# The four conversions in the first second product: PSUM scratch, GpSimd for the remainders, and a later, denser second attention

## The chip, the cores and the metric

The kernel runs on one NeuronCore of a Trainium2 chip. The metric is the device time of one execution in microseconds; the time before is the median of three runs. All times below are microseconds (us) unless marked ns. PE is TensorE, PEld its weight loads, DVE is VectorE, ACT is ScalarE, POOL is GpSimd, SP the queue that issues DMAs.

## The reference, cut to what matters

Causal windowed attention (window 128, linear bias per head) over 8 batches, 8 heads, 576 positions and 64 dimensions, followed by a two-layer network with a Mish activation:

```python
attn = softmax(mask(scale * q @ k.T + bias))      # per batch and head
x = (attn @ v).transpose(0, 2, 1, 3).reshape(4608, 512)
h = x @ w_in                                       # 512 -> 2048
g = h * tanh(softplus(h))                          # Mish
out = g @ w_out                                    # 2048 -> 512
```

The two weight matrices arrive as 64-bit floats, so the kernel turns their bits into 32-bit floats itself, and then splits each 32-bit value into an upper and a lower part for TensorE.

## The kernel before, in words

The rows of x are worked on in chunks: chunk c (0 to 7) is the first 512 positions of batch c, and a ninth chunk holds the remaining 64 positions of all batches. For each chunk there are two stages. The **first product** makes h in eight steps j, each with a [128, 2, 512] PSUM tile of tag `s` (two slots of two banks each), and `mish` turns it into g. The **second product** is 32 **pieces** (`second`): piece 2m+t adds six matmuls of 512 columns to the accumulator bank `po0` or `po1`; m counts 0 to 15, that is two halves of the chunk with j from 0 to 7 in each. Each m needs the two parts of g, made by `parts`: a copy on ACT (`gh`) and a subtraction on POOL (`gl`), both in a tile `gg` that has three buffers; `parts` for m is queued at piece 2m - 4.1. During the second product of chunk c the attention of batch c+1 is computed, so that x is ready when the next first product begins.

An attention is eight **units** (`unit`: a pair of heads, half of the positions), and four short `last_unit`s that go with the even ones. A unit needs one `s` slot. Its steps, with their places in slots after the unit's start: `scores` (0, PE), `exps` (0.02 and 0.25, four times DVE and then ACT), `fold` (0.7, POOL, and two tiny DVE operations), `scale` (0.95, DVE), `weights` (1.3, PE transposes and a DVE masking), `values` (1.99, PE), and for odd units `split_x` (2.02, ACT and then DVE). Units follow one another at one slot's distance; what a slot is in pieces is set by the line that the diff changes.

Every engine runs its instructions in the order in which they were written (the class `InOrder`); this order comes from sorting all steps of a stage by their place in pieces. An instruction that waits holds all that come after it on its engine.

The **conversion** of a quarter matrix (`convert_w`), in two halves a of 512 columns, is four steps: `scaled` (ACT multiplies the high words, into a scratch t), `joined` (three DVE operations on raw words, t and a scratch u: a shift, a shift with an or, a mask with an or), `upper` (ACT copies to the upper part, tile `so` or `si`) and `lower` (a subtraction, engine `last`, POOL unless told otherwise). In the first product of chunk 0 ten quarters are converted (`conv[2:12]`), with t in banks `po0` and `po1` and u in banks `w` and `o`. The last four (`conv[12:]`, the quarters o4 to o7 of w_out) are converted in the second product of chunk 0, which needs o4 in piece 8, o5 in piece 10, o6 in piece 12 and o7 in piece 14. There t lies in SBUF, in a `gg` buffer, u lies in place in the raw words, and `lower` runs on DVE. Banks `w` and `o` are used there by `last_unit` and by `values`.

The upper and lower parts of a quarter lie in the big pool of 20 slots, which are handed on in turn: the tile of quarter o4 gets the slot of raw o3, that of o5 the slot of raw o4, and so on; so `upper` of a quarter has to wait for `lower` of the quarter before it.

All instructions that go through `InOrder` show one line, L30, in the trace, so they are told apart by tile.

Of the kernel before, what the change touches and what calls it, by code (L numbers as in the profile page):

```python
# [8 lines left out]
F32 = mybir.dt.float32  # L9
F32R = mybir.dt.float32r  # L10
U32 = mybir.dt.uint32
# [5 lines left out]
P = 128  # L17
# [18 lines left out]
def attention_mish_mlp(  # L36
# [35 lines left out]
    ps = ctx.enter_context(tc.tile_pool(name="ps", bufs=1, space=bass.MemoryType.PSUM))  # L72
# [17 lines left out]
    for t in vb:  # L90
# [3 lines left out]
    pe, dve, act, pool, sp = (  # L94
        InOrder(tc, e) for e in (nc.tensor, nc.vector, nc.scalar, nc.gpsimd, nc.sync)
    )
# [7 lines left out]
    def big(name, dtype):  # L104
        return wts.tile([P, 2048], dtype, tag="w", name=name, bufs=2 * NJ + NF // 4)
# [4 lines left out]
    def load_w(kind, j):  # L110

        n = 256 if kind == "i" else DM
        if kind == "i":
            src = w_in[:, j * 256 : (j + 1) * 256].rearrange("(c p) f -> p c f", p=P)
        else:
            src = w_out[j * 256 : (j + 1) * 256, :].rearrange("(c p) f -> p c f", p=P)
        if (kind, j) == last_w:

            halves = [
                xp.tile([P, 1024], U32, tag=f"x{NCC - 2 + a}", name=f"w{kind}{j}_{a}")  # L120
                for a in range(2)
            ]
        else:
            t = big(f"w{kind}{j}", U32)
            halves = [t[:, :1024], t[:, 1024:]]
        raw_w[(kind, j)] = halves
        for a, t in enumerate(halves):
            part = src[:, a * (512 // n) : (a + 1) * (512 // n), :]
            if bits:
                load(t.rearrange("p (c n) -> p c n", n=2 * n), part.bitcast(U32))  # L130
            else:
                load(t[:, :512].bitcast(F32).rearrange("p (c n) -> p c n", n=n), part)

    def convert_w(kind, j, banks, last=pool):

        halves = raw_w.pop((kind, j))
        st = {}

        def value(a):
            return halves[a][:, 1::2].bitcast(F32) if bits else halves[a][:, :512].bitcast(F32)

        def place(a, part):
            return split[(kind, j)][:, 1024 * a + 512 * part : 1024 * a + 512 * part + 512]

        def scaled(a):  # L150
            if a == 0:
                split[(kind, j)] = big(f"s{kind}{j}", F32R)
            if not bits:
                return
            if banks:
                st[a] = ps.tile([P, 512], F32, tag=banks[a][0], name=f"t{kind}{j}_{a}")
            else:
                if a == 0:
                    st["t"] = ff.tile([P, 1024], F32, tag="gg", name=f"t{kind}{j}", bufs=3)
                st[a] = st["t"][:, 512 * a : 512 * (a + 1)]  # L160

            act.activation(st[a], value(a), AF.Copy, scale=2.0**-112)

        def joined(a):
            if not bits:
                return
            low, high, tb = halves[a][:, 0::2], halves[a][:, 1::2], st[a].bitcast(U32)
            u = high
            if banks:
                u = ps.tile([P, 512], F32, tag=banks[a][1], name=f"u{kind}{j}_{a}").bitcast(U32)  # L170
            dve.tensor_scalar(out=u, in0=tb, scalar1=3, scalar2=None, op0=ALU.logical_shift_left)
            dve.scalar_tensor_tensor(
                out=high, in0=low, scalar=29, in1=u, op0=ALU.logical_shift_right, op1=ALU.bitwise_or,
            )
            dve.scalar_tensor_tensor(
                out=high, in0=tb, scalar=0x80000000, in1=high, op0=ALU.bitwise_and,
                op1=ALU.bitwise_or,
            )

        def upper(a):  # L180
            act.activation(place(a, 0), value(a), AF.Copy)

        def lower(a):
            last.tensor_tensor(
                out=place(a, 1), in0=value(a), in1=place(a, 0).bitcast(F32), op=ALU.subtract
            )

        return scaled, joined, upper, lower

    def w_part(kind, j, part, c):  # L190
# [262 lines left out]
    def first(c, j, blocks=range(NCC)):  # L453
        if blocks[0] == 0:
            hs[j % 2] = ps.tile([P, 2, CH], F32, tag="s", name=f"h{c}_{j}", bufs=2)
        h = hs[j % 2]
        for t, cc in (
            [(t, cc) for cc in blocks for t in range(2)] if len(blocks) < NCC
            else [(t, cc) for t in range(2) for cc in blocks]
        ):  # L460
            x = xt[(c, cc)]
            for k, (w_, x_) in enumerate(((0, 0), (0, 1), (1, 0))):
                pe.matmul(
                    h[:, t, :], lhsT=w_part("i", j, w_, cc)[:, t * P : (t + 1) * P],
                    rhs=x[:, x_, :], start=(cc == 0 and k == 0), stop=(cc == NCC - 1 and k == 2),
                )
# [3 lines left out]
    def mish(c, j):  # L470
        if j % 2 == 0:
            gt[(c, j // 2)] = big(f"g{c}_{j // 2}", F32).rearrange("p (f n) -> p f n", n=CH)
        f = 2 * (j % 2)
        act.activation(gt[(c, j // 2)][:, f : f + 2, :], hs[j % 2], AF.Mish)
# [3 lines left out]
    def parts(c, half, j):  # L478

        src = gt[(c, j // 2)][:, 2 * (j % 2) : 2 * (j % 2) + 2, half * 256 : (half + 1) * 256]  # L480
        gg = ff.tile([P, 2, 2, 256], F32R, tag="gg", name=f"gg{c}_{half}_{j}", bufs=3)
        gh, gl = gg[:, 0], gg[:, 1]
        act.activation(gh, src, AF.Copy)
        pool.tensor_tensor(out=gl, in0=src, in1=gh.bitcast(F32), op=ALU.subtract)
        gs[(c, half, j)] = (gh, gl)
# [53 lines left out]
    def run(steps):  # L539
        for _, work in sorted(steps, key=lambda s: s[0]):  # L540
            work()

    def converting(weights, times, banks, last=pool):

        steps = []
        for (kind, j), at_ in zip(weights, times):
            st = []
            steps.append((at_[0], lambda kind=kind, j=j, st=st: st.extend(convert_w(kind, j, banks, last))))
            steps += [(t, lambda n=n, st=st: st[n // 2](n % 2)) for n, t in enumerate(at_)]
        return steps  # L550
# [31 lines left out]
    for c in range(B + 1):  # L582

        steps = []
        for j in range(NJ):
            if c or j:
                steps.append((j, lambda j=j: first(c, j)))
            steps.append((j + 0.9, lambda j=j: mish(c, j)))
        steps += [(NJ - 1.05, lambda j=j: parts(c, 0, j)) for j in range(2)]
        if c == 0:  # L590
            steps += converting(
                conv[2:12],
                [
                    [-0.5 + 0.84 * n + d for d in (0, 0.42, 0.3, 0.72, 0.75, 1.15, 0.8, 1.2)]
                    for n in range(10)
                ],
                (("po0", "w"), ("po1", "o")),
            )
        run(steps)
        if c == 0:  # L600
            load_w(*last_w)

        n = 4 * NJ
        steps = []
        for m in range(2 * NJ):
            for t in range(2):
                steps.append((2 * m + t, lambda m=m, t=t: second(c, *divmod(m, NJ), t)))
            if m >= 2:
                steps.append((2 * m - 4.1, lambda m=m: parts(c, *divmod(m, NJ))))
        if c == 0:  # L610
            steps += converting(
                conv[12:],
                [
                    [-0.3 + 2.0 * n + d for d in (0, 0.4, 0.7, 1.5, 1.5, 2.4, 1.9, 2.6)]
                    for n in range(4)
                ],
                None, dve,
            )
        if c + 1 < B:

            t0 = 0 if c else 5
            steps += [(t0 + (n - 2 - t0) / 9.0 * s - 0.2, f) for s, f in attention(c + 1)]
        elif c + 1 == B:
            steps.append((4.5, last_x))
        run(steps)
# [63 lines left out]
```

## Time and profile before

| What | us |
|---|---|
| Median of three runs (1044.23 to 1045.45) | 1044.44 |
| The profiled execution, its own time | 1047.03 |
| Its span, first to last instruction | 1045.3 |
| PE busy in the span | 1002.5 (96%) |
| DVE busy | 367.0 (35%) |
| ACT busy | 395.9 (38%) |
| POOL busy | 292.0 (28%) |

A busy share is a mean over the whole span. The second product of chunk 0 runs from 109.65 to 199.07 in the profiled execution, that of chunk 1 from 242.75 to 310.47.

### The profile page before, as it was taken

To read this page: it belongs to the slowest core of one execution; us is meant where nothing else is said; L and a number is where in the kernel's file an instruction comes from. 1 tells how busy PE (TensorE), PEld (TensorE's weight loads), DVE (VectorE), ACT (ScalarE), POOL (GpSimd) and SP (SyncE) were. 2 spreads that over 40 slices of the span, in tenths; PEclk is the share of its full clock that TensorE was granted. 3 is DMA by queue.
4 is the path that set the end of the run, shared out by engine and by line. 5 is a ranking of instruction groups with operands and counts; after the bars stand their busy time and mean duration, and the time that the engine had idled before them with its cause. 6 is when DMAs were issued, how large, how long until landed. Compare 5 with 4: busy or idle time off the path is not lost.

```text
span 1045.3 us, 14263 instructions
## 1 busy us (share of the span) xinstructions
PE 1002.5 (96%) x5358; PEld 789.3 (76%) x5358; DVE 367.0 (35%) x1118; ACT 395.9 (38%) x958; POOL 292.0 (28%) x286
## 2 busy tenths in 40 slices
PE   7599859999999999999999999999999999999998
PEld 5378547787778777887788777877787778888886
DVE  4879876203540255005610553035402550010000
ACT  4447645215431444234512542154314442231221
POOL 2326434103420243014400341034302430141042
PEclk9789979999999999999999999999999999999999
DMA  8950102200220012002200122003200101010001
GB/s 268 399 182 1 64 6 90 69 0 27 92 70 1 25 60 73 32 1 62 93 33 1 43 77 69 1 26 93 70 1 23 60 14 41 1 41 21 1 1 41
DMA packets 52133, 59.32 MB, mean 57 GB/s; under 512 B 13024, under 2 KB 32608, under 8 KB 52064
## 3 DMA queue, kind: packets, MB, share of 16 engines
q1 hardware_dynamic: 50880, 57.69, 17.2%
q8 instruction: 42, 0.69, 0.3%
q10 hardware_dynamic: 1184, 0.72, 0.2%
q14 instruction: 27, 0.22, 0.1%
HBM read 47.91 MB, written 10.49 MB: 56 GB/s over the span
## 4 chain that ended last, share of the span: by engine, by line
PE 83%; DVE 1%; ACT 1%; POOL 0%; issue 0%; POOLq 0%
PE po L30 36%; PE h L30 33%; PE s L30 8%; PE o L30 4%; DVE pz L30 0%; POOL gg L30 0%; PE pt_1l L30 0%; PE pt_2l L30 0%; PE pt_3l L30 0%; PE pt_0l L30 0%; ACT pz L30 0%; POOL pz L30 0%; ACT gg L30 0%; ACT x L30 0%; ACT pz_3l L30 0%
## 5 line engine op out<-in xcount | busy, mean ns | idle before, releaser
L30 PE MATMUL po<-so,gg 128*128 128x512 f32 x1728 | 430.6, 399 | 2.0 <-ACT gg L30 1.0
L30 PE MATMUL h<-x,si 128*128 128x512 f32 x1728 | 394.6, 390 | 0.0
L30 PEld LDWEIGHTS h<-x,si 128*128 128x128 f32 x1728 | 325.0, 188 | 67.7 <-issue 0.2
L30 POOL TENSOR_TENSOR gg<-g,gg 128x512 fp32r<-128x512 f32 x144 | 185.6, 1292 | 674.6 <-ACT gg L30 570.1
L30 PEld LDWEIGHTS po<-so,gg 128*128 128x128 f32 x1728 | 314.9, 188 | 75.8 <-issue 6.5
L30 DVE CUSTOM_DVE_ANT_0 pz<-s,nb 128x256 f32<-128x256 f32 (+1 forms) x256 | 84.5, 386 | 299.1 <-PE s L30 289.5
L30 ACT ACTIVATE g<-h 128x1024 f32<-128x1024 f32 x72 | 74.0, 1028 | 269.1 <-PE h L30 269.1
L30 ACT ACTIVATE pz<-pz,mx 128x256 f32<-128x256 f32 (+1 forms) x256 | 120.5, 472 | 131.2 <-DVE mx L30 131.1
L30 ACT ACTIVATE gg<-g 128x512 fp32r<-128x512 f32 x144 | 88.5, 622 | 44.7 <-PE po L30 42.8
L30 DVE TENSOR_TENSOR pz<-s,masks 128x1024 f32<-128x1024 f32 x56 | 68.5, 1223 | 21.1 <-PE s L30 21.1
L30 DVE TENSOR_TENSOR pz<-pz,s 128x512 f32<-128x512 f32 x64 | 43.8, 685 | 86.8 <-POOL pz L30 86.4
L30 POOL TENSOR_TENSOR pz<-pz 128x256 f32<-128x256 f32 x64 | 65.1, 1018 | 23.4 <-ACT pz L30 13.4
L30 PE MATMUL s<-qk 64*128 64x128 f32 (+1 forms) x448 | 57.7, 376 | 0.0
L30 PE MATMUL o<-pz,va 128*64 128x128 f32 (+1 forms) x560 | 54.9, 325 | 1.0 <-DVE pz L30 0.9
L30 PEld LDWEIGHTS o<-pz,va 128*64 128x64 f32 x560 | 33.3, 136 | 29.0 <-issue 10.9
L30 DVE COPY ob<-po 128x512 f32<-128x512 f32 x18 | 12.4, 691 | 117.3 <-PE po L30 117.3
L30 PE MATMUL s<-ident,pz 128*128 128x128 f32 x224 | 34.1, 275 | 15.5 <-DVE pz L30 14.4
L30 ACT ACTIVATION_READ_ACCUMULATOR pz<-pz,mx 128x1 f32 x256 | 47.9, 187 | 0.0
L30 PEld LDWEIGHTS s<-ident,pz 128*128 128x128 f32 x224 | 27.8, 141 | 23.5 <-ACT pz_0l L30 14.0
L30 PEld LDWEIGHTS s<-qk 64*128 64x128 f32 x448 | 33.9, 186 | 11.2 <-issue 8.2
L30 ACT ACTIVATE x<-o 128x512 fp32r<-128x512 f32 x32 | 18.8, 588 | 61.6 <-PE o L30 61.2
L30 DVE TENSOR_TENSOR x<-o,x 128x512 fp32r<-128x512 f32 x32 | 22.1, 691 | 54.1 <-ACT x L30 54.1
(122 smaller groups left out, 487.4 us busy)
## 6 DMA issues: line engine op xcount, KB each, us to landing
wi<-in_moe_w_in_dram SPq DMA_DIRECT2D x16, 512.0 KB, 10.8
wo<-in_moe_w_out_dram SPq DMA_DIRECT2D x16, 512.0 KB, 10.5
out_dram<-ob SPq DMA_DIRECT2D x32, 256.0 KB, 2.0
qk<-in_q_dram SPq DMA_DIRECT2D x28, 288.0 KB, 3.4
qk<-in_k_dram SPq DMA_DIRECT2D x28, 288.0 KB, 3.6
va<-in_v_dram SPq DMA_DIRECT2D x28, 256.0 KB, 2.8
first<-in_q_dram SPq DMA_DIRECT2D x4, 288.0 KB, 3.8
first<-in_k_dram SPq DMA_DIRECT2D x4, 288.0 KB, 3.9
```

What stands on the lines that cost most here:

```text
L30: return self.tc.keep_in_program_order(method(*args, **kwargs))
```

## The change: what it does

Three things, all in the second product of chunk 0. The four conversions get their scratch in PSUM: t in bank `w` for half 0 and bank `o` for half 1, and u in a tile of tag `s`, one for both halves; and since no engine is named for `lower`, it runs on POOL. Their places are new: a quarter every 3.05 pieces from -0.8 instead of every 2.0 from -0.3. The attention of batch 1 begins at piece 11 instead of piece 5, and since it ends at the same place, its slots are 19/9 = 2.11 pieces long instead of 25/9 = 2.78.

```diff
             if banks:
-                u = ps.tile([P, 512], F32, tag=banks[a][1], name=f"u{kind}{j}_{a}").bitcast(U32)
+                if banks[a][1] == "s":
+                    if a == 0:
+                        st["u"] = ps.tile([P, 2, 512], F32, tag="s", name=f"u{kind}{j}", bufs=2)
+                    u = st["u"][:, a, :].bitcast(U32)
+                else:
+                    u = ps.tile([P, 512], F32, tag=banks[a][1], name=f"u{kind}{j}_{a}").bitcast(U32)
...
             steps += converting(
                 conv[12:],
                 [
-                    [-0.3 + 2.0 * n + d for d in (0, 0.4, 0.7, 1.5, 1.5, 2.4, 1.9, 2.6)]
+                    [-0.8 + 3.05 * n + d for d in (0, 1.0, 0.5, 2.0, 1.9, 3.3, 2.0, 3.4)]
                     for n in range(4)
                 ],
-                None, dve,
+                (("w", "s"), ("o", "s")),
             )
         if c + 1 < B:
 
-            t0 = 0 if c else 5
+            t0 = 0 if c else 11
             steps += [(t0 + (n - 2 - t0) / 9.0 * s - 0.2, f) for s, f in attention(c + 1)]
```

The eight places in the list of a quarter are, in order: `scaled` of half 0 and 1, `joined` of 0 and 1, `upper` of 0 and 1, `lower` of 0 and 1.

## Rows read from the trace of the kernel before

**Rows 1.** Stretches: length, busy time (instructions) per engine, granted PE clock, DMA.

```profile
core 0: us, PE busy (x) PEld busy (x) DVE busy (x) ACT busy (x) POOL busy (x), PEclk, DMA share, GB/s
109.65:199.07 89.42, 71.02 (x421) 52.29 (x422) 61.04 (x161) 42.33 (x115) 31.91 (x29) 0.92 0.19 61
242.75:310.47 67.72, 67.72 (x421) 51.78 (x422) 36.31 (x126) 31.95 (x97) 26.75 (x26) 1.00 0.22 65
127.78:141.40 13.62, 0.01 (x1) 0.03 (x1) 11.73 (x30) 6.26 (x18) 2.87 (x3) 0.60 0.00 0
```

**Rows 2.** Timeline of PE: start, length, instruction, in brackets the idle time before.

```profile
111.61 5.74 PE L30 MATMUL po<-so,gg 128*128 128x512 f32 x24 [0.34 <-DVE wo L30]
...
117.28 0.93 PE L30 MATMUL s<-qk 64*128 64x128 f32 x8
...
141.40 1.09 PE L30 MATMUL s<-ident,pz 128*128 128x128 f32 x4 [13.61 <-DVE pz L30]
...
199.07 1.29 PE L30 MATMUL h<-x,si 128*128 128x512 f32 x5
```

**Rows 3.** Stretches of 2 us around PE's return; columns as in rows 1.

```profile
142.00:144.00 2.00, 2.00 (x8) 1.71 (x7) 1.23 (x8) 1.77 (x6) 0.08 (x1) 0.50 0.00 0
144.00:146.00 2.00, 2.00 (x9) 1.43 (x8) 1.56 (x2) 1.91 (x6) 1.75 (x2) 0.96 0.00 0
```

**Rows 4.** The chain that ended last, by time: the last chunk's second product.

```profile
997.22 43.53 PE po L30 x192
```

**Rows 5.** A group of DVE instructions, 78 to 112 us: count, busy us, mean ns.

```profile
L30 DVE TENSOR_SCALAR uo<-to 128x512 uint32<-128x512 uint32 x8 | 5.5, 692 | 1.1 <-ACT to L30 1.0
```

**Rows 6.** Timeline of DVE, end of the first product and of the conversions.

```profile
110.86 0.69 DVE L30 SCALAR_TENSOR_TENSOR wo<-to,wo 128x512 uint32<-128x512 uint32 x1
113.70 1.09 DVE L30 TENSOR_SCALAR wo<-to 128x512 uint32<-128x512 uint32 x1 [2.14 <-ACT to L30]
...
118.93 0.68 DVE L30 TENSOR_TENSOR so<-wo,so 128x512 fp32r<-128x512 f32 x1
...
125.17 2.38 DVE L30 TENSOR_TENSOR so<-wo,so 128x512 fp32r<-128x512 f32 x2
```

**Rows 7.** Timeline of ACT.

```profile
110.97 0.68 ACT L30 ACTIVATE so<-wo 128x512 fp32r<-128x512 f32 x1 [2.54 <-POOL so L30]
...
113.00 0.67 ACT L30 ACTIVATE to<-wo 128x512 f32<-128x512 f32 x1
...
126.54 1.28 ACT L30 ACT_TABLE_LOAD   x1
...
158.42 0.51 ACT L30 ACTIVATE pz<-pz,mx 128x256 f32<-128x256 f32 x1 [1.10 <-DVE mx L30]
...
160.41 0.62 ACT L30 ACTIVATE gg<-g 128x512 fp32r<-128x512 f32 x1
```

**Rows 8.** Timeline of POOL.

```profile
113.19 1.31 POOL L30 TENSOR_TENSOR so<-wo,so 128x512 fp32r<-128x512 f32 x1
...
125.40 1.60 POOL L30 TENSOR_TENSOR gg<-g,gg 128x512 fp32r<-128x512 f32 x1 [4.28 <-ACT gg L30]
...
161.16 1.27 POOL L30 TENSOR_TENSOR gg<-g,gg 128x512 fp32r<-128x512 f32 x1 [4.75 <-PE po L30]
162.38 1.27 POOL L30 TENSOR_TENSOR pz<-pz 128x512 f32<-128x512 f32 x1
```

**Rows 9.** Timeline of DVE: `scale` of units 2 to 5, and one `split_x`.

```profile
156.16 0.69 DVE L30 TENSOR_TENSOR pz<-pz,s 128x512 f32<-128x512 f32 x1 [2.25 <-POOL pz L30]
157.36 0.69 DVE L30 TENSOR_TENSOR x<-o,x 128x512 fp32r<-128x512 f32 x1 [0.51 <-ACT x L30]
...
163.69 0.69 DVE L30 TENSOR_TENSOR pz<-pz,s 128x512 f32<-128x512 f32 x1 [1.91 <-POOL pz L30]
...
167.93 0.67 DVE L30 TENSOR_TENSOR pz<-pz,s 128x512 f32<-128x512 f32 x1
...
177.05 0.69 DVE L30 TENSOR_TENSOR pz<-pz,s 128x512 f32<-128x512 f32 x1 [2.51 <-POOL pz L30]
```

## Prediction

> **What bounds the kernel now.** I read the busy shares first: TensorE is busy for 96% of the span, so a change pays only where PE stands still or runs slowly. Then the stretches [rows 1]: the second product of chunk 0 takes 89.42, that of chunk 1, with the same 421 products, 67.72, with PE busy throughout. So 21.70 is all that the changed stage can return. The PE timeline [rows 2] shows where most of it lies: one wait of 13.61 before the transposes of unit 0, released by DVE (`scale` of unit 0). During it PE's clock falls: a mean of 0.60 over 13.62 is full speed for about 2.7 after PE stopped and half speed, 1.2 GHz, from then on [rows 1]; after PE's return at 141.40 it stays at 0.50 until about 144 [rows 3], so some 2.7 of products run at half speed, a loss of 1.35. PE's idle time in the stage is 89.42 - 71.02 = 18.4, so there are 4.8 of other, shorter waits. 21.70 - 18.4 - 1.35 leaves about 2 of products merely drawn out around the waits.
>
> DVE explains the long wait: it is busy for 11.73 of those 13.62 [rows 1]. Its queue holds the conversions ahead of the `exps` and the `scale` of unit 0.
>
> **The change, part by part.** A piece is 43.53 / 32 = 1.36 of PE [rows 4]. An attention costs PE 67.72 - 43.53 = 24.2, or 3.0 per unit [rows 1, 4].
>
> *DVE.* With u in PSUM the three operations of `joined` have the form of the first product's: 0.69 each [rows 5, 6], 2.07 for a half, 16.6 for the eight. In the old form the shift is in SBUF; one took 1.09 at 113.70 [rows 6], while POOL was in a subtraction [rows 8]. The eight subtractions leave DVE: undisturbed 0.68, two beside POOL 2.38 together [rows 6], so some 8 in all. The start doesn't move: DVE ends the first product's work at 111.55 and waits for the first `scaled`, on ACT from 113.00 [rows 6, 7], behind an `upper` that waited 2.54 for POOL [rows 7]. DVE thus has the last `joined` done at 113.7 + 16.6 = 130.3, if nothing holds it. It needs ACT alone, whose scaled halves stay ahead: at most two copies and one `gg` of about 0.6 each come between.
>
> *POOL.* This is the new long queue. It is busy with the first product's last `lower` until 114.5 [rows 8]. Its order then is `gl` of m=2, lower, `gl` 3, lower, `gl` 4, lower, lower, `gl` 5, lower, `gl` 6, lower, `gl` 7, lower, lower, `gl` 8, `fold` of unit 0. At 1.31 for a `lower` and 1.28 for a `gl` [rows 8], with about 0.75 of waiting for the first `upper` (ready at 115.75 + 0.66), `gl` 5 is done at 125.5 and the seventh `lower` at 132.0. The eighth waits for its `upper`, which ACT has queued behind `exps` of unit 0: the seventh `upper` done at 130.1, the table load for Exp 1.28 [rows 7], four exponentials of at most 2.0 (158.42 to 160.41) [rows 7], the `upper` 0.66: about 133.9. So lower to 135.2, `gl` 8 to 136.5, `fold` of half the width to 137.2, and `scale` (0.69 [rows 9]) to 137.9.
>
> *PE.* Piece 1 starts at 111.61 as now, after a wait of 0.34 [rows 2], for a bank that the first product's conversions hold. Thirteen pieces, two `scores` (0.93 for the eight short products [rows 2]; about 1.4 with the `last_unit`'s and 1.1 for the second), and 0.8 in piece 10 for `gl` 5, give 111.61 + 17.7 + 2.5 + 0.8 = 132.6. PE has to wait there until 137.9: 5.3 in place of 13.61. This is longer than the 2.7 for which the clock held out in the old wait, so I keep its 1.35. The quarters themselves are in time: o4, o5 and o6 are wanted in the third product of pieces 8, 10 and 12, at about 121.6, 124.4 and 129.4, and their last `lower` ends at 120.4, 124.3 and 129.4; o7 is ready at 135.2, before PE's return.
>
> *Banks and transfers.* The first `s` slots come free when `mish` of the last steps has read h, before DVE needs them; `scores` of units 0 and 1 take the slots of o6's and o7's u, free by 126 and 129.6, when PE gets there. The loads of the later pairs and their v move with the units (piece 7.7 to 13.0 for the first, on SP's queue, beside the stores of pieces 14 and 15). Each lands within 4 (medians 2.8 to 3.6 in the profile's DMA issues) and is used over six pieces later, more than 8: nothing.
>
> *Shorter slots.* PE needs 2.11 x 1.36 + 3.0 = 5.9 per slot; with 2.78 it was 6.8. Against this stands a loop over engines: `scale` of one unit, then DVE's `exps` of the next, ACT, POOL's `fold`, `scale`. From unit 2 to 3 it took 163.69 - 156.16 = 7.53 [rows 9], with `split_x` (about 1.2) at its start and a `gg` copy and a `gl` (together 1.9, 160.41 to 162.38) [rows 7, 8] before the `fold`. In the new order a `gg` and `gl` stand before the `fold` of units 0 to 5. So the loop is 7.5 to units 3 and 5, about 6.3 to unit 1, 5.6 to units 2 and 4 (narrower exponentials and fold), and 1.3 to 1.9 less to units 6 and 7. PE's own slots alternate between 6.0 and 5.2, but 7.4 from unit 4 to 5, where three pieces fall, and 4.7 to unit 7. Walked through, PE waits 0.3, 1.5, 0.2, 0.1 and 0.9: 3.0.
>
> *Sum.* 0.34 + 0.8 + 5.3 + 1.35 + 3.0, and 1.0 of products drawn out (half of the 2 above, as the waits are about half), is 11.8 over the undisturbed 67.72, where it was 21.7. The stage becomes 9.9 shorter: in the profiled execution 1047.03 would become 1037.1 and the span 1035.4. The median of the runs is 1044.44, 2.6 below that execution; from it, **1034.5**.
>
> **A rule that speaks against one part.** A subtraction of two 128x512 tiles takes 1.31 on POOL [rows 8] and 0.68 on DVE [rows 6] where nothing disturbs it. The Trainium skill, GPSIMD Engine Reference, section 4.1, says the same as a rule: elementwise work on a tile belongs on VectorE, since GpSimd is about twice as slow with two inputs. By that rule the change moves eight operations the wrong way, and rival B is the result. But two subtractions on DVE beside a `gl` took 2.38 [rows 6], and the Trainium skill, SBUF — State Buffer, section "SBUF: two separate sides", explains such rows: a DVE operation with two SBUF inputs and a GpSimd operation lock each other out for a whole instruction. All new forms on DVE have an input in PSUM, and the rows of the first product show no such stretching.
>
> **The rivals.**
>
> A, *everything is covered*: `fold` and `scale` come soon after DVE's end, and the loops fit. For it: DVE is done at 130.3, and with exponentials, fold and scale (2.5 + 0.75 + 0.69) behind, unit 0 could be ready at 134.3; without a wait over 2.7 the clock stays full. Against it: the written order of ACT and POOL. Price: only 0.34, perhaps 1.7 and 1 remain, a gain of 21.7 - 3 = 18.7: **1025.7**.
>
> B, *POOL is slower, and the slots don't shorten*: each of the 14 operations ahead of `fold` takes 1.60, as one `gl` beside DVE did [rows 8], which adds 14 x 0.3 = 4.2; and two slots keep the 13.4 that units 3 to 5 took (163.69 to 177.05) [rows 9], 6.7 each over 5.9, another 5.6 for seven, less the 3.0 counted: a gain of 9.9 - 4.2 - 2.6 = 3.1, **1041.3**. Against it: the first product's `lower` keeps 1.31 beside a busy DVE, and PE itself paced the old slots most of the time.
>
> C, *slower*: the loop rules the slots and lengthens them. All that is counted apart from slots is 8.8, so the stage is slower than now once slots cost 12.9 of waits. PE's seven intervals add up to 39.7, so this is reached at a mean loop of 7.5. The loop to unit 5 took 177.05 - 167.93 = 9.1, with 2.51 of it waiting for POOL [rows 9]; if all were so, the waits would be 24 and the time 1044.4 + 11.1 = **1055.5**. Against it: PE was late in most of those loops, and the one to unit 4 took 4.2, 13.4 for both [rows 9].
>
> That the change does nothing is excluded by the same stretch: DVE's queue before unit 0 changes by some 8.
>
> **How the numbers follow.** Forecast (1030.5 to 1038) 0.58; A, towards 1025.7, 0.15; B, 1038 to 1042.4, 0.18; C or no change 0.09. The range 1025.5 to 1041.5 runs from A to B: the wait at unit 0 between 1.7 and 9.5, those of the slots between 0 and 5.6; what lies beyond is C and the tails. 0.2% is about 2.1 us, which is what a measurement of this kernel can tell from no change: 0.91 faster, 0.04 the same, 0.05 slower.
>
> **What the profile would show.** DVE's `joined` in 0.69s from 113.7 to about 130.3, without subtractions; POOL without a pause from 115 to 132; the long wait of PE at 132 to 138, before the first transposes, released by a DVE that waits for POOL; the clock down in it; the steps from one `scale` to the next near 7.5 and 5.6 in turn; the first product of chunk 1 from about 189. The prediction is wrong if PE waits earlier, for `so` of o4 to o7; if `exps` of unit 0 come much after 131; or if PE waits over 1.5 in most slots.

## The result, and the profile after

The changed kernel takes 1035.93 (median of four runs, 1034.06 to 1036.46) against 1044.91 in the runs beside it: a ratio of 0.9906, 95% interval 0.9894 to 0.9919. That is 9.0 less; the forecast was 9.9 less, 1034.5. The span of the profiled execution fell from 1045.3 to 1034.5.

The moment at which the second product of chunk 0 begins differs by up to 2.8 between the profiles of this document, and by 1.1 between two profiles of the changed kernel (109.42 and 108.34). Kernels are therefore compared below by the **stage**: from the start of piece 0 to the first product of chunk 1, on PE's timeline. It was 89.42 [rows 1]. Now, as a stretch, and stretches of 2 us in PE's wait and after it (columns as in rows 1):

```profile
109.42:188.34 78.92, 70.79 (x421) 52.67 (x422) 53.69 (x153) 42.20 (x115) 40.59 (x37) 0.98 0.22 69
...
134.00:136.00 2.00, 0.00 (x0) 0.00 (x0) 0.33 (x2) 0.51 (x1) 2.00 (x2) 1.00 0.28 93
136.00:138.00 2.00, 0.31 (x2) 0.34 (x3) 1.15 (x4) 0.48 (x2) 1.09 (x3) 0.91 0.00 0
138.00:140.00 2.00, 2.00 (x8) 1.78 (x7) 2.00 (x8) 2.00 (x9) 0.00 (x0) 0.50 0.03 8
140.00:142.00 2.00, 2.00 (x8) 1.56 (x7) 0.96 (x3) 0.52 (x1) 1.41 (x2) 0.73 0.00 0
```

The stage is 10.5 shorter; the rest of the span's 10.8 lies in its beginning. DVE has 7.4 less to do in it, POOL 8.7 more. PE's timeline after:

```profile
111.38 13.47 PE L30 MATMUL po<-so,gg 128*128 128x512 f32 x58 [0.34 <-DVE wo L30]
125.38 0.73 PE L30 MATMUL po<-so,gg 128*128 128x512 f32 x2 [0.52 <-POOL gg L30]
...
137.69 1.09 PE L30 MATMUL s<-ident,pz 128*128 128x128 f32 x4 [4.66 <-DVE pz L30]
...
138.64 4.14 PE L30 MATMUL po<-so,gg 128*128 128x512 f32 x12
...
145.48 3.00 PE L30 MATMUL po<-so,gg 128*128 128x512 f32 x12
...
158.46 0.63 PE L30 MATMUL s<-ident,pz 128*128 128x128 f32 x4 [1.28 <-DVE xo_1l L30]
...
188.34 16.94 PE L30 MATMUL h<-x,si 128*128 128x512 f32 x74
```

The wait of 13.61 [rows 2] has become 4.66, at the same transposes, and five more pieces are done before it. The granted clock stays at 1.00 through the whole wait and falls only as PE comes back. The twelve products behind it still take 4.14, where 3.00 is usual (at 145.48), since the clock is then at half until about 141. What the wait hangs on is seen on POOL and ACT:

```profile
130.34 1.29 POOL L30 TENSOR_TENSOR so<-wo,so 128x512 fp32r<-128x512 f32 x1
133.63 1.29 POOL L30 TENSOR_TENSOR so<-wo,so 128x512 fp32r<-128x512 f32 x1 [2.00 <-ACT so L30]
134.88 1.26 POOL L30 TENSOR_TENSOR gg<-g,gg 128x512 fp32r<-128x512 f32 x1
136.09 0.72 POOL L30 TENSOR_TENSOR pz<-pz 128x256 f32<-128x256 f32 x1
```
```profile
129.84 1.28 ACT L30 ACT_TABLE_LOAD   x1
...
132.91 0.64 ACT L30 ACTIVATE so<-wo 128x512 fp32r<-128x512 f32 x1
```

ACT makes the last `upper` behind the table load and four exponentials; POOL waits 2.00 for it, does the last `lower`, then `gl` of m=8, and only then the `fold` of unit 0. Two of the three DVE operations of `joined` in this stage, grouped (count, busy us, mean ns), and the same two in the kernel before; the third, the mask with an or, takes 5.5 in both:

```profile
L30 DVE TENSOR_SCALAR uo<-to 128x512 uint32<-128x512 uint32 x8 | 5.5, 692 | 2.1 <-ACT to L30 2.1
...
L30 DVE SCALAR_TENSOR_TENSOR wo<-wo,uo 128x512 uint32<-128x512 uint32 x8 | 5.5, 689 | 0.3
```
```profile
L30 DVE SCALAR_TENSOR_TENSOR wo<-wo 128x512 uint32<-128x512 uint32 x8 | 6.5, 815 | 0.3
...
L30 DVE TENSOR_SCALAR wo<-to 128x512 uint32<-128x512 uint32 x8 | 4.6, 569 | 2.1 <-ACT to L30 2.1
```

So `joined` takes 16.5 in all with its scratch in PSUM and took 16.6 before: the shift became longer on average (the 1.09 of rows 6 is the longest of eight), the shift with an or shorter. What DVE has less to do is the eight subtractions, 8.3 before.

And `scale` of units 0 to 7, on DVE, to be read against rows 9:

```profile
136.85 0.69 DVE L30 TENSOR_TENSOR pz<-pz,s 128x512 f32<-128x512 f32 x1 [2.46 <-POOL pz L30]
...
143.15 0.69 DVE L30 TENSOR_TENSOR pz<-pz,s 128x512 f32<-128x512 f32 x1 [0.73 <-POOL pz L30]
...
150.16 0.69 DVE L30 TENSOR_TENSOR pz<-pz,s 128x512 f32<-128x512 f32 x1 [1.25 <-POOL pz L30]
...
157.62 0.69 DVE L30 TENSOR_TENSOR pz<-pz,s 128x512 f32<-128x512 f32 x1 [2.44 <-POOL pz L30]
...
163.15 0.69 DVE L30 TENSOR_TENSOR pz<-pz,s 128x512 f32<-128x512 f32 x1 [1.21 <-POOL pz L30]
...
170.63 0.69 DVE L30 TENSOR_TENSOR pz<-pz,s 128x512 f32<-128x512 f32 x1 [2.45 <-POOL pz L30]
...
175.17 0.69 DVE L30 TENSOR_TENSOR pz<-pz,s 128x512 f32<-128x512 f32 x1 [0.19 <-POOL pz L30]
...
181.68 0.69 DVE L30 TENSOR_TENSOR pz<-pz,s 128x512 f32<-128x512 f32 x1 [1.23 <-POOL pz L30]
```

The steps are 6.30, 7.01, 7.46, 5.53, 7.48, 4.54 and 6.51; before each `scale` DVE waits for POOL.

### The profile page after: what moved, and what is told of

Same layout as the page of the kernel before. It is cut to its first block, busy times and chain, and to the rows that moved or that the text cites. A ratio compares the mean times of both kernels' runs of the same rounds, so it can differ in the third digit from the quotient of the medians.

```text
span 1034.5 us, 14272 instructions
## 1 busy us (share of the span) xinstructions
PE 999.0 (97%) x5358; PEld 787.4 (76%) x5358; DVE 359.5 (35%) x1110; ACT 395.7 (38%) x958; POOL 300.6 (29%) x294
## 4 chain that ended last, share of the span: by engine, by line
PE 87%; issue 3%; DVE 2%; ACT 2%; POOL 2%; POOLq 0%; DVEq 0%; ACTq 0%
PE h L30 37%; PE po L30 36%; PE s L30 8%; PE o L30 5%; ACT pz L30 1%; POOL pz L30 1%; DVE wo L30 1%; POOL gg L30 1%; POOL so L30 1%; DVE wi L30 0%; DVE pz L30 0%; DVE uo L30 0%; ACT so L30 0%; PE pt_0l L30 0%; PE pt_2l L30 0%
## 5 line engine op out<-in xcount | busy, mean ns | idle before, releaser
L30 PEld LDWEIGHTS s<-qk 64*128 64x128 f32 x448 | 33.9, 186 | 11.2 <-issue 8.2
## 6 DMA issues: line engine op xcount, KB each, us to landing
wi<-in_moe_w_in_dram SPq DMA_DIRECT2D x16, 512.0 KB, 10.8
```

The lines of the kernel that those rows point to most:

```text
L30: return self.tc.keep_in_program_order(method(*args, **kwargs))
```

## The experiments

The theory: the gain comes from DVE's shorter queue and the later begin together; what is left of the wait is POOL's queue in front of `fold`, with the clock's fall behind it; in the short slots `gl` in front of `fold` costs PE another 2.4. The rivals: POOL is the wrong home for the remainders; one part of the change does it alone; PE itself sets the pace. Each run, with the median, the ratio to the kernel before on the same chip, and the stage:

| Run | us | ratio (95%) | stage |
|---|---|---|---|
| changed kernel | 1035.93 | 0.9906 (0.9894 to 0.9919) | 78.92 |
| e1, lower on DVE | 1041.28 | 0.9967 (0.9954 to 0.9979) | 85.04 |
| e2, old conversions, late begin | 1043.64 | 0.9991 (0.9982 to 1.0) | 88.42 |
| e3, gl just behind fold | 1034.86 | 0.9904 (0.9891 to 0.9918) | 78.18 |
| e4, last upper and lower early | 1034.40 | 0.9910 (0.9896 to 0.9925) | 78.89 |
| e5, gl between the next exps | 1029.24 | 0.9853 (0.9832 to 0.9873) | 73.03 |
| e6, gl twice | 1045.22 | 0.9999 (0.999 to 1.0008) | 88.94 |
| e7, PE kept busy | 1039.24 | 0.9942 (0.993 to 0.9955) | 82.55 |
| e8, e4 and e5 together | 1028.74 | 0.9843 (0.9828 to 0.9857) | 72.21 |
| e9, PE kept busy, free bank | 1034.24 | 0.9896 (0.988 to 0.9913) | 77.46 |
| changed kernel, beside e9 | 1036.42 | 0.9918 (0.9903 to 0.9933) | 79.07 |

**e1: the remainders on DVE again.**

```diff
-                (("w", "s"), ("o", "s")),
+                (("w", "s"), ("o", "s")), dve,
```

> The changed kernel with the eight remainders (lower) of o4 to o7 on DVE again; scratch in PSUM and all places as changed. Theory (POOL is the better home while DVE's queue holds back unit 0): DVE gets 8 subtractions of 0.68 to 1.3 on top of 16.5 and waits for ACT before some, so its conversions end near 136 to 138 instead of 130, scale of unit 0 near 140 to 141 instead of 137.5, the wait of PE before the first transposes grows from 4.66 to 7 to 9; time about 1038 to 1041. Rival (elementwise work belongs on VectorE, POOL was the bound): unit 0 is ready sooner, the wait shrinks to under 3.5, time under 1034.

The stage is 6.1 longer than with POOL; PE's waits, and DVE's subtractions:

```profile
133.19 1.13 PE L30 MATMUL s<-qk 64*128 64x256 f32 x8 [1.57 <-DVE wo L30]
142.01 1.09 PE L30 MATMUL s<-ident,pz 128*128 128x128 f32 x4 [6.10 <-DVE pz L30]
```
```profile
L30 DVE TENSOR_TENSOR so<-wo,so 128x512 fp32r<-128x512 f32 x8 | 6.4, 820 | 1.7 <-ACT so L30 1.7
```

`scale` of unit 0 came at 141.2, just past the expected 140 to 141, although this stage began 1.1 earlier. The first wait grew to 6.10 only, where 7 to 9 was expected, as PE was held at three more places before it, among them the `scores` of unit 1, whose slot DVE's last `joined` still used. The time of 1041.28 is just over the expected 1038 to 1041. The rival is out: a subtraction is faster on DVE (0.82 with its neighbours' disturbance, 1.3 on POOL), and the kernel slower.

**e2: the later begin alone.** The conversions as in the old lines of the diff ahead of the prediction, `None, dve` with the old places, and t0 = 11.

> The changed kernel with the conversions of o4 to o7 as they were before (t in a gg buffer, u in place, remainders on DVE, a quarter every 2.0 pieces); only the attention's later begin and its 2.11 slots remain. Theory (PSUM scratch with POOL and the later begin are both needed): DVE's conversions end near 138 to 140, unit 0 is ready near 143 to 145, so PE waits 10 to 12 before the transposes, with 5 more pieces done than in the kernel before; time 1039 to 1043. Rival 1 (the later begin alone does it): wait under 6, time within 2 of the changed kernel's 1035.9. Rival 2 (the old conversions starve the pieces of gg buffers, as t takes them): new waits for gg of over 3 in pieces 4 to 12, time at 1044 or over.

The time is 1043.64, a gain of only 0.1%, and the upper end of its interval is at 1. Both mechanisms are in the trace: unit 0 is late (PE returns at 144.97, after a wait of 4.74 where 10 to 12 was expected), and the pieces starve, as rival 2 said, with 5.3 of waits for `gg` copies on ACT in three places, none as long as 3:

```profile
123.98 1.20 PE L30 MATMUL po<-so,gg 128*128 128x512 f32 x4 [2.08 <-ACT gg L30]
...
144.97 1.08 PE L30 MATMUL s<-ident,pz 128*128 128x128 f32 x4 [4.74 <-DVE pz L30]
```
```profile
L30 DVE TENSOR_TENSOR so<-wo,so 128x512 fp32r<-128x512 f32 x8 | 10.0, 1254 | 1.0 <-ACT so L30 0.7
```

So nearly all of the gain needs the conversions' new form. Against e2, e1 has the scratch and the new places alone, which no run separates: they take 3.4 off the stage. PE's waits for `gg` copies fall from 5.3 to 0.9, as t no longer takes `gg` buffers, and the subtractions on DVE from 10.0 to 6.4. Moving these to POOL takes off another 6.1. The other half, the new form with the old begin at piece 5, was not tried: u would take `s` slots between those of unit 0 and unit 1, and by the written order PE would come to the `scores` of unit 1 before the work that frees their slot. So that the later begin is needed as well is argued from the order, not shown by a run.

**e3: gl just behind fold.**

```diff
-                steps.append((2 * m - 4.1, lambda m=m: parts(...)))
+                at_ = 2 * m - 4.1
+                if c == 0 and m >= NJ:
+                    at_ = 10.8 + 19 / 9 * (m - NJ + 0.72)
+                steps.append((at_, lambda m=m: parts(...)))
```

> The changed kernel with the g parts (gg on ACT, gl on POOL) of the second half, m = 8 to 15, queued just behind the fold of units 0 to 7 instead of just before it. Theory (the gl in front of fold lengthens the loop from one scale to the next): scale of unit 0 1.2 sooner, the wait before the first transposes 3.4 instead of 4.66; the loops to units 1 to 5 about 1.3 shorter, the later waits (2.4 in sum) under 1; time 2 to 4 below the changed kernel, 1032 to 1034. Rival (PE paces the slots): only the first 1.2, and a part of gl comes late for its piece; time 1035 or over.

The first wait is 3.44, as expected; the stage fell by 0.7 alone, and the time of 1034.86 is above the expected 1032 to 1034. The waits in the slots didn't vanish, they moved from the transposes to `values`:

```profile
136.73 0.64 PE L30 MATMUL s<-ident,pz 128*128 128x128 f32 x4 [3.44 <-DVE pz L30]
...
154.46 0.87 PE L30 MATMUL o<-pz,va 128*64 128x256 f32 x8 [0.64 <-DVE pz L30]
166.61 0.87 PE L30 MATMUL o<-pz,va 128*64 128x256 f32 x8 [0.83 <-DVE pz L30]
179.52 0.87 PE L30 MATMUL o<-pz,va 128*64 128x256 f32 x8 [1.48 <-DVE pz L30]
```
```profile
150.29 0.40 ACT L30 ACTIVATE pz_1l<-pz_1l,sm_1l 128x128 f32<-128x128 f32 x1 [1.66 <-POOL pz_1l L30]
```
```profile
151.20 0.69 DVE L30 TENSOR_TENSOR x<-o,x 128x512 fp32r<-128x512 f32 x1 [2.11 <-ACT x L30]
```

The theory of the loop was too narrow. Behind `fold`, `gl` stands in front of the `last_unit`'s fold on POOL; ACT waits 1.66 for that one before `split_x`, DVE waits 2.11 for ACT, and the next `exps` and the masking are queued behind it. The old kernel had this too, in its loop of 9.1 to unit 5 [rows 9], with the same waits of 1.66 on ACT and 2.11 on DVE. `gl` has to be behind `split_x` as well, which e5 tries.

**e4: the last upper and lower before the exps of unit 0.**

```diff
-d in (0, 1.0, 0.5, 2.0, 1.9, 3.3, 2.0, 3.4)
+d in (0, 1.0, 0.5, 2.0, 1.9, *((3.3, 2.0, 3.4) if n < 3 else (2.4, 2.0, 2.41)))
```

> The changed kernel with the last upper and lower of o7 queued before the exps of unit 0 instead of behind them. Theory (fold of unit 0 waits for gl of m=8, and this for its gg copy on ACT, behind exps): the last lower is done 2 sooner, but gl and fold hardly move; wait before the first transposes 4.2 to 4.9, time within 1 of the changed kernel. Rival (the last lower itself holds fold back): the wait falls by 1.3 or more, time under 1034.5.

The wait is 4.79 and the stage 78.89, unchanged. POOL is done with the last `lower` early and then waits for the `gg` copy, which ACT has behind the exponentials:

```profile
132.57 1.26 POOL L30 TENSOR_TENSOR gg<-g,gg 128x512 fp32r<-128x512 f32 x1 [2.09 <-ACT gg L30]
```

The median of 1034.40 lies 1.5 below the changed kernel's, but on another chip; the ratios to the kernel before, 0.9910 and 0.9906, show no difference.

**e5: gl behind split_x.** As e3, with 1.03 in place of 0.72: behind `fold`, the last unit's fold and `split_x`, between the two `exps` of the next unit.

> The changed kernel with the g parts of m = 8 to 15 queued at 1.03 slots after the start of units 0 to 7, that is behind fold, the last unit's fold and split_x, between the two exps steps of the next unit. Theory (a gl in front of fold lengthens the loop from scale to scale, and one in front of the last unit's fold holds back split_x and the next exps just as long): scale of unit 0 1.2 sooner, and the waits behind the first fall from 2.4 to under 0.8; the stage, 78.9 from its first piece to the next first product, becomes about 75.3, the time 1032 to 1033. Rival (PE or DVE sets the pace of the slots, wherever gl lies): the waits move on to another place as in the run with gl just behind fold, stage over 77.5.

The stage is 73.03, 5.9 shorter, where 3.6 was expected; after the wait before the first transposes PE has no wait left that the timeline shows. 1.2 comes from unit 0, 2.4 from the slots, and some 1.5 from the clock, as e9 below prices it, which I had not counted on; the remaining 0.8 is fewer products drawn out. The clock didn't fall in a wait of 3.45 (the wait, and 2 us after it):

```profile
130.42:133.87 3.45, 0.01 (x1) 0.04 (x1) 1.52 (x6) 1.37 (x4) 2.25 (x3) 1.00 0.43 156
...
134.00:136.00 2.00, 2.00 (x12) 1.74 (x12) 2.00 (x9) 1.90 (x6) 0.21 (x1) 1.00 0.00 0
```

**e6: the suspect doubled.**

```diff
         pool.tensor_tensor(out=gl, in0=src, in1=gh.bitcast(F32), op=ALU.subtract)
+        if c == 0 and half == 1:
+            pool.tensor_tensor(out=gl, in0=src, in1=gh.bitcast(F32), op=ALU.subtract)
```

> The changed kernel in which POOL does the subtraction of gl twice for m = 8 to 15 (same operands, same result), so that what stands in front of fold costs 1.27 more. Theory (POOL's queue before fold sets unit 0 and the pace of the units): the first long wait grows by 1.3, and five or six of the loops by 1.3 each less their slack; stage 78.9 plus 5 to 7.5, time 1041 to 1043.5. Rival (PE sets the pace, POOL has room): only the first wait grows, stage plus 1 to 2, time under 1038.

Eight more operations of 1.27 on an engine that is busy for half of the stage lengthen it by 10.0, as long as they are: PE's waits grow by 7.7, and the clock, low for longer, and drawn-out products make up the rest. That is more than the 5 to 7.5 expected, and clearly not PE's pace. All of the change's gain is gone:

```profile
137.20 0.69 DVE L30 TENSOR_TENSOR pz<-pz,s 128x512 f32<-128x512 f32 x1 [3.80 <-POOL pz L30]
...
190.69 0.69 DVE L30 TENSOR_TENSOR pz<-pz,s 128x512 f32<-128x512 f32 x1 [2.57 <-POOL pz L30]
```

From the first `scale` to the eighth it is 53.5, a mean loop of 7.6, and the time equals that of the kernel before. Rival C of the prediction set the point of no gain at 7.5.

**e7 and e9: PE kept busy in the wait.**

```diff
+        if c == 0:
+            steps.append((13.53, lambda: busy(36, places[1, 0][:, 1, 256:])))                        # e7
+            steps.append((13.53, lambda: busy(36, ps.tile([P, 512], F32, tag="w", ...)[:, : 2 * P])))  # e9
```

> The changed kernel with 36 small products (256 columns, bf16, into a part of unit 0's bank that nobody reads any more) on PE between piece 13 and the first transposes, some 3.9 long and so inside the wait of 4.66. Theory (the fall of PE's clock in the wait costs 1.35, and the engines behind are early enough to let PE use them): granted clock 1.00 throughout, pieces 14 and 15 in 2.75 instead of 4.14, stage 77.4 to 77.8, time 1034 to 1035. Rival (after the wait the loop over DVE, ACT and POOL sets the pace): the clock holds, the time doesn't move, stage 78.6 or over.

```profile
135.10 5.53 PE L30 MATMUL s<-masks 128*128 128x256 bf16 x36 [4.58 <-DVE pz L30]
```

This run missed its purpose: the small products were released by DVE's `scale` like the transposes, so the whole wait lay ahead of them, and they added 3.6 to the stage. In a bank that nobody else used at that time:

> As the run that kept PE busy, with the 36 small products into bank w, which nobody uses at that time, so that they no longer wait for scale of unit 0. Theory (the fall of the clock in the wait costs 1.35, and the engines behind are early enough): products run from about 133 to 137 after the stage began at 109.4, 1.0 of idle time is left, granted clock 1.00, pieces 14 and 15 in 2.75; stage 77.4 to 77.9 instead of 78.9, time about 1.2 below the changed kernel of the same chip. Rival (the loop over DVE, ACT and POOL sets the pace after the wait): the clock holds, stage 78.6 or over, the time the same.

```profile
131.66 4.11 PE L30 MATMUL idle<-masks 128*128 128x256 bf16 x36
136.50 0.67 PE L30 MATMUL s<-ident,pz 128*128 128x128 f32 x4 [0.74 <-DVE pz L30]
...
137.04 3.01 PE L30 MATMUL po<-so,gg 128*128 128x512 f32 x12
```

The two pieces take 3.01 to their modelled end in place of 4.14, and the stage is 77.46, 1.5 under 78.92 and 1.6 under the changed kernel beside it. So the clock's fall cost 1.5 to 1.6, a little over the 1.35 counted, and the engines behind did let PE use it. The medians differ by 2.2 where 1.2 was expected; the intervals of the ratios overlap, though all four runs of e9 lie below all four of the changed kernel. For the changed kernel beside it:

> The changed kernel once more, unaltered, beside the others on one chip: stage 78.9, time 1034 to 1036.5.

It took 1036.42, stage 79.07.

**e8: both moves.** e4's and e5's edits together.

> The changed kernel with both moves: the g parts of m = 8 to 15 between the exps of the next unit, and the last upper and lower of o7 ahead of the exps of unit 0. Theory (the fold of unit 0 then waits for nothing but its own exponentials): scale of unit 0 2.3 sooner, the wait 2.4 instead of 4.66 and so too short for the clock to fall, the later waits under 0.8; stage about 73, time 1029 to 1031. Rival (another engine is late by then, DVE's end of the conversions for instance): the wait stays over 3.5, the clock falls, stage over 75.

The time is 1028.74, the stage 72.21; all that PE waits for in it, 106.93 to 179.14 (us in total, times, longest):

```profile
PE s L30 <- DVE pz L30: 2.6, 1, 2.6
PE po L30 <- POOL gg L30: 0.6, 1, 0.6
PE po L30 <- DVE wo L30: 0.3, 1, 0.3
```

The last `lower`, which changed nothing by itself, gives 0.8 here, as `gl` no longer hides it. Its ratio of 0.9843 is the lowest: the interval lies below that of the changed kernel, but overlaps that of e5, so that between these two no difference in the time is shown.

## Why the prediction was right

*What the stage can return.* From the first `scores` to the next first product, chunk 1 takes 67.62 in the changed kernel (231.95 to 299.57) and 67.63 in the old one, so the measure of the undisturbed stage holds; 421 products are in both. So 11.2 of the old 21.7 are left; predicted were 11.8.

*From the stage to the time.* The stage became 10.5 shorter where 9.9 was forecast, and the profiled execution came to 1036.27 for 1037.1. The median is 1.4 above the forecast all the same, since the prediction set it 2.6 below the profiled execution, as in the old kernel, and it was 0.3 below. Such distances come largely from the beginning: the two profiles of the changed kernel differ by 0.92 in time, by 1.08 in the begin of the stage and by 0.15 the other way in its length.

*DVE.* Its conversions ran from 113.41 to 130.07 with the operations at 0.69; forecast were 113.7 and 130.3. The 1.09 that the prediction set beside them was the longest of the old shifts: `joined` as a whole is no shorter, and DVE's relief is the subtractions alone. That leaving them on DVE costs more was shown by e1, that the begin alone isn't enough by e2.

*POOL and ACT.* The walk through the written order gave the seventh `lower` to 132.0, the last to 135.2, `fold` to 137.2 and `scale` to 137.9; the trace has 131.6, 134.9, 136.8 and 137.5, in a stage that began 0.23 earlier. The wait was 4.66 for 5.3, as PE came to it 0.4 after the forecast 132.6.

*The clock.* Counted at 1.35; by e9 it was 1.5 to 1.6. The reason given was too simple, and that the term came out is in part luck. The prediction took the 2.7 for which the clock had held out in the old wait as the bound, and expected the clock to be down in the new one. It held out for the whole 4.66 and fell as PE came back; it did not fall in or after e5's wait of 3.45, and it did after a wait of 2.61 in e6 (last section). In the old kernel the long wait followed 1.03 and 0.49 of others within 4 us; in the changed one PE had waited only 0.52 in the 20 us before it. No run shows whether that made the difference.

*The slots.* 3.0 was counted for the waits, and 2.4 measured (0.43, 1.28, 0.26, 0.20, 0.21). The loops to units 3 and 5 took 7.46 and 7.48 for 7.5, the one to unit 1 6.30 for 6.3, the one to unit 4 5.53 for 5.6. But the one to unit 2 took 7.01 for 5.6: before its `exps` DVE waited 1.24 for PE's `scores`, which the low clock had made late. In e9, where the clock held, it took 5.58. The picture of the loop was incomplete too: e3 showed that `gl` can hold back the next `exps` by way of the last unit's fold and `split_x`. In the change's own order DVE waits for POOL's `fold` before each `scale`, so the sum didn't suffer.

*Drawn-out products.* The shown waits, 0.34 + 0.52 + 4.66 + 2.4, with 1.5 for the clock, are 9.4 of the 11.2; so 1.8 is drawn out where I took 1.0. This term was too small by 0.8, and the waits, 7.9 where 9.4 was counted, more than covered it. So the sum is closer than its terms.

*The rivals.* A, everything covered, did not happen, but e8 comes to about 3 above its 1025.7 after two changes of order. B failed on both halves: POOL kept 1.3 beside DVE, and the slots' waits were 2.4 for its 5.6, though the two slots to unit 5 took 13.0, hardly less than the old 13.4. (B counts 14 operations ahead of `fold`; its own list, and the trace, have 15, which would add 0.3 to its price.) The rule of the Trainium skill, GPSIMD Engine Reference, section 4.1, that elementwise work belongs on VectorE, holds for one operation here and not for the kernel: e1 follows it and is 5.3 slower. C is real as a mechanism, as e6 shows, with its point of no gain about where it was put; the change stays at a mean loop of 6.4.

## What to carry to other kernels

Where engines run in a written order, walk each queue past the wait that is to go: here DVE's work fell by 7, and the wait ended where POOL's and ACT's order let it, which such a walk gave to within 1 us. Choose the engine of an operation by whose queue stands in front of the critical step, not by who does it faster. When an operation is moved out of a loop, look at what stands behind its new place too: `gl` just behind `fold` returned 0.7, a third of a slot further 5.9, some 1.5 of it by way of the clock, without any work being saved.

## What the runs showed of the hardware

The length of a single wait of PE did not tell whether the clock would fall. After 3.45 in e5 and after 2.62 in e8 the granted clock stayed at 1.00. After 2.61 in e6 it fell, 1.2 after PE's return (PE's line, then a stretch of 2 us):

```profile
162.09 0.63 PE L30 MATMUL s<-ident,pz 128*128 128x128 f32 x4 [2.61 <-DVE xo_1l L30]
```
```profile
164.00:166.00 2.00, 2.00 (x6) 1.59 (x5) 1.28 (x7) 1.18 (x5) 1.22 (x1) 0.50 0.01 1
```

In e2 it fell just behind a wait of 2.09, the third in 13 us after 1.09 and 2.08 (0.57 from 130 to 132). In e3 it fell after 3.44 and a second wait of 0.48 close behind, which e5 does not have:

```profile
137.85 0.48 PE L30 MATMUL pt_0l<-ident,pz_0l 128*128 128x128 f32 x1 [0.48 <-ACT pz_0l L30]
```
```profile
136.00:138.00 2.00, 0.80 (x6) 0.59 (x6) 2.00 (x10) 0.61 (x2) 1.36 (x2) 0.89 0.04 8
138.00:140.00 2.00, 2.00 (x6) 1.61 (x7) 1.42 (x2) 2.00 (x9) 0.16 (x1) 0.50 0.00 0
```

So in these runs waits of 2.1 to 3.5 cost their own time alone in some places, and the clock besides, some 1.5 by e9, in others. The Trainium skill, TensorE: Matmul & The Clock Gate, section "What's actually happening", says that the hardware's watch over PE runs free of the kernel, so that the point of a change varies; e6 and e8 agree with that, though none here shows the watch itself, and in e2 and e3 the neighbouring waits may have counted as well.

A change of the activation tables cost ACT 1.30 from the end of one instruction to the start of the next (129.84 to 131.14 after the change), no more than the load's own 1.28.
